# Residual of the S5 output tiles added by the copying engine, with a new task order

## The chip, the cores and the metric

The kernel runs on one core of a Trainium2 chip. A core has five engines that take their own instruction queues in order: TensorE (PE, matrix products; its weight loads are shown apart as PEld), VectorE (DVE), ScalarE (ACT), GpSimd (POOL) and SyncE (SP), which here only issues DMA transfers. Engines wait for each other through semaphores. Products land in PSUM, eight banks of 512 fp32 numbers for each of 128 partitions; DVE and ACT copy them from there to SBUF, the working memory.

The metric is the device time of one execution in microseconds. Three runs of the kernel before gave 341.81, 342.16 and 343.07; the median is 342.16.

## What is computed

One sequence of 2048 tokens with 640 channels passes four layers: A, B, A, B. Weights are shared between the two A layers and between the two B layers, and B's inputs k and v are given, not computed from x.

```
x = x + A(layernorm(x))      # S5: h_t = Lam*h_{t-1} + B u_t ; y = 2 Re(C h_t) + D*u
x = x + B(layernorm(x))      # H3: kv = shift_conv(k)*v ; y = q*(fft_conv(kv, ssm_k) + kv*ssm_D)
x = x + A(layernorm(x))
x = x + B(layernorm(x))
```

In A, u is the normalised x, h a complex state of 640 channels, and the last step of a tile adds three things: the product of state and output matrix, the skip term D*u, and the residual x. In B, q is the normalised x, and the long convolution does not depend on x, so it is computed once for both layers. The output is bf16.

## The kernel before, in words

**Stages.** The first part of the kernel prepares: tables for the Fourier transforms (`yt_`), the products k*v (`kv_`), the S5 matrices in two forms for even and odd steps (`a_b0`, `a_b1`, `a_w1`, `a_wc`, `a_wm`, tables `a_t`), and five passes over 128 channels each, `yq0` to `yq4`, that compute B's convolution: forward transform of kernel (`KA`, `KB`) and data (`VA`, `VB`), a product on DVE (`pw`), and the inverse (`IB`, `IA`), with transposes by DMA (`vl`, `tt`) between. The result goes to a DRAM scratch `ysd` (`st`). Each of these products is an `m` task on PE with an `e` task beside it that copies the bank out.

Then the layers A1, B1, A2, B2 work on four chunks `c0` to `c3` of 512 tokens. An A chunk has these tasks:

- `ln_*`, `id:q` normalise, `tu` transposes by DMA;
- `bq`, `bp` multiply by B for odd and even steps (PE), `eq`, `ev` copy out;
- `ri` turns the phases so that the scan becomes real, `sc` scans, `cy` hands the state to the next chunk, `ro` turns back, `hx` forms the even states: all on DVE, all strictly one after another;
- `cp:q` is the output product of one tile of 128 tokens (PE, two banks), `xe:q` copies it out into `x` and sums it for the next layernorm.

The last chunk (`QUADS`) handles four tokens at a step, with shorter scans and additional small products `b4` and `h1` and their copies `e2` and `eh`. `a_tq`, `a_rq` and `a_lamd2` make its tables. A B chunk has `ln_*`, `u` (normalise), `mm` (multiply by the convolution), `m` (add the residual) and, in B2, `st` (store).

**The residual of a tile.** Chunks of A1 reload x in bf16 (`xr`); chunks of A2 have it in SBUF in fp32. `PE_RES` lists the chunks of A1 and `XE32` the chunks of A2 where PE adds it: `e_cp` then ends each of its two column groups (512 and 128) with a product of an identity with x, in bf16 for A1 and in fp32 for A2's last chunk. These are all four chunks of A1 and chunk 3 of A2. For such tiles `e_xe` is a plain copy with a running sum, on ACT (line 900) or on DVE (line 902). For the chunks 0 to 2 of A2 `e_xe` is always on DVE and adds x in the same instruction (line 904).

**The order.** Nothing is scheduled at run time. `ORDER` is a list of 907 task names, written out by an earlier planner; `Sched.run` emits them one by one, so the list is the order of every engine's queue, SP's among them. A letter behind a name picks the engine where there is a choice (`/a` ACT, `/d` DVE, `/p` POOL). `PLACE` gives each buffer its place in one large SBUF arena (units of 64 bytes) or its PSUM bank; a buffer may overlap an earlier one, whose readers it then waits for. The estimates beside the tasks do not affect the emitted program.

**Warm-up.** `e_warm` fills PE's time before its first input with 72 products of the identity with itself, 128 columns each.

Of the kernel before, what the change touches and what calls it, by code (L numbers as in the profile page):

```python
# [9 lines left out]
ALU = mybir.AluOpType  # L10
# [7 lines left out]
P = 128  # L18
L = 2048
D = 640  # L20
# [15 lines left out]
PE_RES = (0, 1, 2, 3)  # L36
QUADS = (3,)
XE32 = (3,)
# [20 lines left out]
ORDER = """  # L59
warm yt_io8 yt_ph8 a_ldB0 yq0_kl a_ldB1 a_b00:4 kv_kd a_pl kv_dsl kv_lk0 kv_lv0 a_b00:1 a_b00:2 yt_sin8 yt_f0 kv_pd2/p  # L60
a_ti yt_h0 kv_pd0/d yt_f2 yt_f3 yt_io0 yt_h1 yq1_kl kv_lk1 xl0 kv_lv1 yt_ph0 kv_pd1/d kv_d0 a_p0 yt_neg8 kv_pd4/d
kv_k0 yt_f4 a_p1 yt_sin0 a_b0e0:4/a yt_neg0 a_p2 a_b0e0:1/a a_b00:3 kv_k1 kv_d1 a_b01:3 yt_h2 a_p3 a_b0e0:2/d a_dd
a_b0e1:3/a a_b0e0:3/d kv_d2 kv_k2 yq0_ka kv_ds0 kv_ds2 kv_ds4 kv_ds3 kv_ds1 yt_h3/p kv_pd3/p a_b01:2 a_b01:0
a_b0e1:0/a a_b0e1:2/d a_b00:0 a_b0e0:0/a a_p4a a_p4 yq0_KA:m0 yq0_KA:m3 yq0_KA:m1 kv_mm0:1 yq0_KA:e1/d yq0_KA:e0/a
yq0_KA:e3/a a_p5a yq0_KA:m2 yq0_KA:e2/a kv_ev0:1 a_ta a_p5b a_b01:4 a_b0e1:4/d kv_mm0:0 yq0_KB:m2 kv_ev0:0 yq1_ka
yq0_KB:e2/d yq1_KA:m2 a_t0 yq1_KA:e2/a yq0_KB:m0 yq1_KA:m3 yq0_KB:m3 yq0_KB:e0/a yq1_KA:e3/a yq0_vl a_ldC0 yq1_KA:m1
yq1_KA:e1/a a_ldC1 yq0_KB:e3/d a_p6 a_lamd yt_Si yt_Ci xl2 kv_lk2 kv_lv2 yq2_kl a_b01:1 kv_mm1:1 kv_ev1:1 a_b0e1:1/a
kv_mm1:0 kv_ev1:0 a_t1 yq1_vl kv_lk3 yq0_KB:m1 a_b11:1 a_b1e1:1/d a_b11:0 a_b10:1 kv_lv3 a_b11:3 a_b1e0:1/a a_b1e1:3/a
yq0_KB:e1/d a_b1e1:0/a A1c0_ln_bn:3/d yq0_VA:m2 yq0_VA:e2/d yq0_VA:m3 yq0_VA:m1 yq0_VA:e1/d yq0_VA:e3/a yq0_VA:m0
a_b11:4 a_b1e1:4/d yq0_VA:e0/a yq1_KA:m0 a_f A1c0_ln_bn:1/d A1c0_ln_bn:0/d a_b10:4 yq1_KA:e0/a a_b1e0:4/a yq0_VB:m0  # L70
a_ct1 yq0_VB:m3 yq0_VB:e0/a a_wc01:0 a_wm01:0 yq0_VB:e3/a yq0_VB:m2 yq0_VB:e2/a a_lm2 yt_nsi yt_nci a_wc01:1 a_wm01:1
a_b10:2 yq0_VB:m1 a_b1e0:2/a yq0_VB:e1/a yq0_pw:0 yq1_KB:m1 a_b10:3 yq1_KB:e1/a yq1_KB:m3 a_b1e0:3/a a_b11:2 a_b10:0
yq1_KB:m2 a_b1e1:2/a a_b1e0:0/a yq1_KB:e2/a yq1_KB:e3/a kv_mm2:1 yq0_IB:m1 yq0_IB:m0 kv_mm2:0 A1c0_ln_bn:2/d
A1c0_ln_sd A1c2_ln_bn:0/d kv_ev2:1 yq2_ka A1c0_ln_post A1c0_id:0/d yq0_IB:e1/a A1c0_id:1/d kv_ev2:0 yq1_KB:m0 a_t2
A1c0_id:2/d yq0_IB:e0/a A1c0_id:3/a yq1_KB:e0/a yq2_KA:m3 yq1_VA:m2 yq0_IB:m3 yq2_vl yq2_KA:m0 yq2_KA:e3/a yq1_VA:e2/a
yq2_KA:e0/d yq1_VA:m1 yq1_VA:m0 A1c2_ln_bn:3/d A1c2_ln_bn:1/d A1c2_ln_bn:2/d yq0_IB:e3/a yq1_VA:m3 yq0_IB:m2
yq1_VA:e0/a yq1_VA:e1/a yq1_VA:e3/a kv_mm3:1 kv_ev3:1 yq0_IB:e2/a yq0_tt A1c2_ln_sd a_ct4 yq1_VB:m1 kv_mm3:0 a_wc04:0
a_wm04:0 A1c2_ln_post yq1_VB:e1/a yq1_VB:m0 a_wc04:1 yq1_VB:e0/a kv_ev3:0 a_wm04:1 yq1_VB:m3 a_ct0 yq1_VB:e3/d
A1c2_id:2/a a_wc00:0 a_wm00:0 A1c2_id:0/d A1c2_id:3/d A1c2_id:1/d yq1_VB:m2 yq1_VB:e2/a a_wc00:1 a_wm00:1 yq0_IA:m1
yq0_IA:e1/a A1c0_tu xl1 yq0_IA:m0 yq2_VA:m3 yq0_IA:e0/a yq1_pw:0 yq0_st yq2_VA:m2 yq2_VA:e3/a yq2_KA:m1 yq2_KA:m2  # L80
yq3_kl kv_lv4 kv_lk4 yq2_VA:e2/a a_ct2 yq2_KA:e1/a yq2_KA:e2/a a_wc02:0 a_wm02:0 yq2_VA:m1 yq3_vl yq2_KB:m0
A1c1_ln_bn:2/d yq2_VA:e1/a yq2_KB:m1 yq2_KB:e0/a a_wc02:1 a_wm02:1 yq1_IB:m0 yq2_KB:e1/a yq1_IB:e0/a A1c1_ln_bn:1/d
yq2_VA:m0 yq2_VA:e0/a A1c1_ln_bn:3/d yq3_ka A1c1_ln_bn:0/d yq1_IB:m3 yq1_IB:e3/a a_ct3 a_wc03:0 yq1_IB:m1 yq1_IB:e1/a
a_wm03:0 yq1_IB:m2 yq1_IB:e2/d yq1_tt A1c1_ln_sd a_wc03:1 a_wm03:1 yq2_KB:m2 yq2_KB:e2/a kv_mm4:1 yq3_KA:m2 kv_mm4:0
yq2_VB:m2 yq3_KA:e2/a yq3_KA:m0 A1c1_ln_post A1c1_id:1/d kv_ev4:1 yq2_VB:m0 A1c1_id:3/a yq3_KA:e0/a kv_ev4:0
yq2_VB:e2/d yq2_KB:m3 yq3_KA:m1 A1c1_id:2/d yq2_VB:m1 yq2_KB:e3/d A1c1_id:0/d yq2_VB:e0/a yq3_KA:e1/d A1c0_bq:2
yq2_VB:m3 yq2_VB:e1/a A1c0_eq:2/a yq3_KA:m3 yq3_VA:m0 A1c0_bp:2 A1c2_tu yq3_KA:e3/d yq2_VB:e3/a yq1_IA:m1 yq2_pw:0
A1c0_bq:1 yq3_VA:e0/a A1c0_ev:2/a yq1_IA:e1/a xl3 A1c0_eq:1/a yq4_kl A1c1_tu yq4_vl A1c3_ln_bn:1/d yq3_KB:m0 yq3_VA:m1
yq3_VA:m2 A1c0_bp:1 yq3_VA:e1/a yq3_VA:e2/a yq3_VA:m3 A1c0_ev:1/d yq3_KB:m3 A1c3_ln_bn:3/d yq4_ka A1c3_ln_bn:0/d
yq3_KB:e0/a yq3_VA:e3/a yq2_IB:m2 yq3_KB:e3/a yq3_KB:m2 yq2_IB:e2/a yq3_KB:e2/a yq3_VB:m2 yq3_VB:e2/a yq2_IB:m0  # L90
yq2_IB:e0/d yq3_VB:m3 yq3_VB:e3/a yq1_IA:m0 yq1_IA:e0/d yq1_st A1c3_ln_bn:2/d yq3_VB:m0 yq4_KA:m2 yq2_IB:m1 yq3_KB:m1
yq3_VB:e0/a yq4_KA:e2/d yq2_IB:m3 yq2_IB:e1/a A1c3_ln_sd yq3_VB:m1 yq2_IB:e3/d A1c3_ln_post A1c3_id:0/d yq3_KB:e1/a
yq3_VB:e1/a A1c3_id:3/d yq3_pw:0 A1c3_id:1/d yq4_KA:m3 yq4_KA:e3/a A1c0_bq:0 yq2_tt yq4_KA:m1 yq4_KA:m0 A1c1_bq:0
A1c0_eq:0/a A1c3_id:2/a yq4_KA:e0/a yq4_KA:e1/a A1c0_bp:0 a_rq A1c0_ev:0/a yq4_KB:m1 A1c2_bq:2 yq3_IB:m3 A1c0_ri
A1c0_sc a_rq2 A1c0_cy A1c0_ro yq4_KB:e1/a yq2_IA:m0 A1c2_eq:2/a A1c1_bq:2 A1c2_bp:2 A1c1_eq:0/a yq3_IB:e3/a
yq2_IA:e0/a yq2_IA:m1 A1c2_ev:2/a A1c1_eq:2/a yq2_IA:e1/a A1c1_bq:1 A1c1_eq:1/a yq2_st A1c1_bp:2 yq4_KB:m2 A1c1_bp:1
yq4_KB:e2/a yq4_VA:m3 yq4_VA:e3/a A1c1_ev:2/a A1c1_ev:1/a A1c1_bp:0 yq3_IB:m1 yq3_IB:m2 A1c1_ev:0/a yq4_VA:m1
yq3_IB:e1/a yq4_KB:m3 yq4_VA:e1/a yq3_IB:m0 A1c2_bq:0 yq3_IB:e2/d A1c1_ri A1c0_hx A1c1_sc A1c1_cy yq3_IB:e0/a
yq4_VA:m2 yq4_VA:m0 yq4_KB:e3/a A1c2_eq:0/a A1c2_bq:1 yq4_VA:e0/a yq4_KB:m0 A1c3_tu A1c0_xr yq4_VA:e2/a A1c2_eq:1/a
yq4_VB:m3 A1c2_bp:0 yq3_tt yq4_VB:e3/a yq4_VB:m1 yq4_KB:e0/a A1c2_ev:0/a yq4_VB:m0 yq4_VB:m2 A1c2_bp:1 yq4_VB:e2/d  # L100
A1c1_xr yq4_VB:e1/a yq4_VB:e0/d yq4_pw:0 A1c0_cp:1 A1c1_ro A1c2_ev:1/a A1c0_xe:1/a a_w10:2 a_w1e0:2/a a_w11:0 a_w10:1
a_w11:4 A1c0_cp:3 a_w1e1:4/a a_w1e0:1/a a_w1e1:0/a yq4_IB:m2 a_w11:3 a_w10:3 A1c0_xe:3/a a_w10:0 yq4_IB:e2/a yq4_IB:m0
a_w1e0:3/a a_w1e1:3/a a_w1e0:0/d yq4_IB:e0/a a_w11:2 yq4_IB:m1 a_w10:4 a_w1e1:2/a yq4_IB:e1/a yq4_IB:m3 a_w1e0:4/d
a_w11:1 yq4_IB:e3/a yq3_IA:m1 yq3_IA:e1/d a_w1e1:1/d A1c1_hx yq4_tt A1c2_ri A1c1_cp:3 A1c1_xe:3/a yq3_IA:m0 A1c0_cp:0
yq3_IA:e0/a A1c3_bq:2 yq4_IA:m1 A1c0_xe:0/a yq4_IA:e1/a A1c0_cp:2 A1c0_xe:2/a A1c3_eq:2/d A1c2_sc A1c2_cy A1c2_ro
yq4_IA:m0 yq4_IA:e0/a B1c0_ln_nm B1c0_ln_sq:2 B1c0_ln_sq:1 A1c1_cp:1 A1c1_xe:1/a B1c0_ln_sq:0 B1c0_ln_sq:3 A1c1_cp:0
yq3_st A1c2_xr yq4_st B1l0 A1c1_cp:2 B1c0_ln_sd B1c0_ln_post B1c0_u:3/d A1c1_xe:0/d A1c2_hx B1c0_u:2/d B1c0_u:0/a
A1c1_xe:2/a B1c1_ln_nm B1c1_ln_sq:3 B1c1_ln_sq:2 B1c1_ln_sq:0 B1c1_ln_sq:1 B1c0_u:1/d B1c0_mm B1c0_m:3 B1c0_m:1
A1c3_bq:0 A1c3_bp:2 A1c2_cp:1 A1c3_bq:1 B1c0_m:2 B1c0_m:0 B1c1_ln_sd B1c1_ln_post a_lamd2 B1c1_u:0/d B1c1_u:1/d
A1c3_eq:0/a A2c0_ln_nm A2c0_ln_sq:1 B1c1_u:3/a B1l2 B1l1 A1c3_bp:0 B1c1_u:2/d B1c1_mm B1c1_m:0 A1c2_xe:1/d  # L110
A2c0_ln_sq:0 A1c3_eq:1/a A2c0_ln_sq:3 A1c3_bp:1 A1c3_e2:2/a A1c3_e2:0/a A2c0_ln_sq:2 A2c0_ln_sd B1c1_m:1 A1c3_b4:2
A1c3_b4:0 A1c2_cp:3 B1c1_m:3 A2c0_ln_post B1c1_m:2 A2c0_id:0/a A1c3_e2:1/a A2c1_ln_nm A1c3_ev:0/d A2c0_id:3/d
A2c0_id:2/d A1c3_ev:2/a A2c0_id:1/a A1c3_b4:1 A2c1_ln_sq:3 A2c0_tu a_tq/d A1c3_ev:1/a A1c3_ri A1c3_sc A1c3_ro
A1c3_hx:1 A1c3_xr A1c2_cp:2 A1c2_xe:3/a A2c1_ln_sq:1 A2c1_ln_sq:0 A1c2_cp:0 A1c2_xe:2/a A2c1_ln_sq:2 A1c2_xe:0/a
B1c2_ln_nm B1c2_ln_sq:2 B1c2_ln_sq:0 B1c2_ln_sq:3 B1c2_ln_sq:1 B1c2_ln_sd B1c2_ln_post B1c2_u:0/d B1c2_u:1/d A2c0_bq:1
A2c0_bq:2 A2c0_eq:1/a A1c3_h1:1 A2c0_bq:0 A1c3_h1:0 A1c3_h1:2 B1c2_u:3/a A2c0_bp:1 B1c2_u:2/d B1c2_mm B1c2_m:1
A1c3_eh:1/d A1c3_eh:0/d B1c2_m:3 A1c3_eh:2/a A2c1_ln_sd A2c0_eq:0/a A2c0_eq:2/a A2c0_ev:1/a A2c0_bp:0 A2c1_ln_post
# [77 lines left out]
    "A2c2_pb0": 6, "A2c2_pb1": 0, "A2c2_pb2": 4, "A2c2_pc0": 6, "A2c2_pc1": 2, "A2c2_pc2": 4, "A2c2_pc3": 0,  # L195
    "A2c3_pb0": 6, "A2c3_pb1": 4, "A2c3_pb2": 2, "A2c3_ph0": 0, "A2c3_ph1": 1, "A2c3_ph2": 6, "A2c3_pc0": 4,
    "A2c3_pc1": 6, "A2c3_pc2": 0, "A2c3_pc3": 2,
}


class Task:
# [1340 lines left out]
```

## Time and profile before

| | before |
|---|---|
| median of 3 runs | 342.16 us |
| profiled execution | 345.72 us |
| its span, first to last instruction | 343.6 us |
| PE busy | 318.2 us (93%) |
| DVE busy | 315.8 us (92%) |
| ACT busy | 248.8 us (72%) |
| POOL busy | 15.3 us (4%) |
| mean granted PE clock | 0.97 |
| DMA moved | 41.6 MB |

The profiled execution is one more run, a little slower than the others; its span leaves out 2.1 us at the ends. A row of a view names the engine, the source line, the operation, output and input, and a count; "busy" of PE counts every product until its modelled end, so that back-to-back products overlap and the start times tell the true rate. The waits are put down to the last releaser. ACT's largest waits are those for the output products, 20.9 us in 11 waits before line 900.

### The profile page before, as it was taken

To read this page: it belongs to the slowest core of one execution; us is meant where nothing else is said; L and a number is where in the kernel's file an instruction comes from. 1 tells how busy PE (TensorE), PEld (TensorE's weight loads), DVE (VectorE), ACT (ScalarE), POOL (GpSimd) and SP (SyncE) were. 2 spreads that over 40 slices of the span, in tenths; PEclk is the share of its full clock that TensorE was granted. 3 is DMA by queue.
4 is the path that set the end of the run, shared out by engine and by line. 5 is a ranking of instruction groups with operands and counts; after the bars stand their busy time and mean duration, and the time that the engine had idled before them with its cause. 6 is when DMAs were issued, how large, how long until landed. Compare 5 with 4: busy or idle time off the path is not lost. (4 is left out here: it accounts for less than half of the span.)

```text
span 343.6 us, 9079 instructions
## 1 busy us (share of the span) xinstructions
PE 318.2 (93%) x3924; PEld 250.9 (73%) x3924; DVE 315.8 (92%) x469; ACT 248.8 (72%) x401; POOL 15.3 (4%) x51
## 2 busy tenths in 40 slices
PE   7776989958899999999999999999999999999992
PEld 7666889857788889887666677676677786776551
DVE  6997997989889899999879999999998999999995
ACT  6897899989779797883745687888474783580772
POOL 6640000000000000000000000000000000000000
PEclk9897899987999999999999999999999999999998
DMA  8999998599959752078064550611416040224023
GB/s 210 242 201 254 228 208 156 100 214 217 189 98 188 166 110 63 2 129 226 0 118 88 167 184 0 155 32 46 88 66 78 3 76 2 76 78 154 2 112 117
DMA packets 105097, 41.61 MB, mean 121 GB/s; under 512 B 97885, under 2 KB 100450, under 8 KB 105058
## 3 DMA queue, kind: packets, MB, share of 16 engines
q1 hardware_dynamic: 104912, 41.03, 55.3%
q8 instruction: 30, 0.49, 0.6%
q14 instruction: 9, 0.07, 0.1%
q10 hardware_dynamic: 146, 0.01, 0.0%
HBM read 19.02 MB, written 5.24 MB: 71 GB/s over the span
## 5 line engine op out<-in xcount | busy, mean ns | idle before, releaser
L288 ACT ACTIVATE arena<-banks 128x1024 bf16<-128x1024 f32 (+3 forms) x155 | 135.3, 921 | 50.7 <-PE banks L756 13.1
L892 PE MATMUL banks<-arena 128*128 128x128 bf16 (+1 forms) x800 | 102.7, 283 | 0.4 <-DVE arena L902 0.4
L892 PEld LDWEIGHTS <-arena 128*128 128x128 bf16 x800 | 61.3, 98 | 42.6 <-issue 2.8
L741 PE MATMUL banks<-arena 128*128 128x256 bf16 x400 | 47.0, 273 | 0.2 <-DMA arena<-arena 0.2
L756 PE MATMUL banks<-arena 128*128 128x256 bf16 x400 | 46.9, 273 | 0.0
L290 DVE CAST arena<-banks 128x1024 bf16<-128x1024 f32 (+3 forms) x35 | 36.2, 1048 | 9.9 <-PE banks L1254 3.2
L756 PEld LDWEIGHTS <-arena 128*128 128x128 bf16 x400 | 38.6, 98 | 4.7
L741 PEld LDWEIGHTS <-arena 128*128 128x128 bf16 x400 | 38.3, 98 | 4.8 <-issue 0.4
L794 DVE TENSOR_TENSOR arena<-arena 128x5160 bf16<-128x5160 bf16 (+1 forms) x16 | 40.2, 2510 | 1.4 <-PE banks L892 1.0
L633 ACT ACTIVATE junk<-arena,nmean 128x640 bf16<-128x640 f32 x48 | 39.6, 826 | 1.1
L1276 PE MATMUL banks<-arena 128*128 128x256 bf16 x160 | 38.5, 279 | 1.3 <-ACT arena L288 1.0
L811 DVE TENSOR_TENSOR_SCAN arena<-arena 128x1290 bf16<-128x1290 f32 (+1 forms) x16 | 39.3, 2498 | 0.2
L1277 PE MATMUL banks<-arena 128*128 128x128 bf16 x160 | 35.7, 223 | 2.9 <-issue 2.9
L1278 PE MATMUL banks<-arena 128*128 128x128 bf16 x160 | 35.7, 223 | 0.0
L687 ACT ACTIVATE arena<-arena,nmr,rstd 128x640 bf16<-128x640 f32 (+1 forms) x25 | 22.4, 912 | 7.6 <-DVE nmr L646 7.1
L900 ACT ACTIVATE arena<-banks 128x640 f32<-128x640 f32 x18 | 12.6, 701 | 21.1 <-PE banks L892 20.9
L1358 PE MATMUL banks<-arena 128*128 128x128 bf16 (+1 forms) x288 | 24.1, 237 | 0.0
L1358 PEld LDWEIGHTS <-arena 128*128 128x128 bf16 x288 | 20.8, 98 | 1.8
L795 DVE TENSOR_TENSOR arena<-arena 128x2580 bf16<-128x2580 bf16 (+1 forms) x16 | 21.4, 1336 | 0.6
L1278 PEld LDWEIGHTS <-arena 128*128 128x128 bf16 x160 | 16.0, 100 | 5.3 <-issue 3.0
L689 DVE TENSOR_SCALAR arena<-arena,rstd,nmr 128x640 bf16<-128x640 f32 (+1 forms) x35 | 18.0, 550 | 0.4
L1277 PEld LDWEIGHTS <-arena 128*128 128x128 bf16 x160 | 15.9, 100 | 1.8 <-issue 1.7
(207 smaller groups left out, 441.5 us busy)
## 6 DMA issues: line engine op xcount, KB each, us to landing
arena<-in_A_x_dram SPq DMA_DIRECT2D x8, 640.0 KB, 4.6
arena<-ysd SPq DMA_DIRECT2D x8, 640.0 KB, 5.0
arena<-in_B_ssm_k_dram SPq DMA_DIRECT2D x5, 512.0 KB, 6.9
arena<-in_B_v_dram SPq DMA_DIRECT2D x5, 512.0 KB, 6.8
ysd<-arena SPq DMA_DIRECT2D x5, 512.0 KB
out_dram<-arena SPq DMA_DIRECT2D x8, 320.0 KB, 2.2
arena<-in_A_B_re_dram SPq DMA_DIRECT2D x1, 800.0 KB, 5.2
arena<-in_A_B_im_dram SPq DMA_DIRECT2D x1, 800.0 KB, 6.8
```

Source lines behind the costliest of these rows:

```text
L288: nc.scalar.activation(out, in_, ACT.Copy)
L290: nc.vector.tensor_copy(out, in_)
L633: nc.scalar.activation(small.junk, src(q), ACT.Square, bias=st["nmean"][:, i:i + 1], scale=1.0, accum_out=st["ssq"][:, i:i + 1])
L741: nc.tensor.matmul(pb[:, jj, c2, :], lhsT=bt0[:, c2, k, j * P:(j + 1) * P], rhs=uT[:, 2:4, k, :], start=(c2 == k == 0), stop=(c2 == 1 and ...
L756: nc.tensor.matmul(pb[:, jj, c2, :], lhsT=bt1[:, c2, j, k, :], rhs=uT[:, 0:2, k, :], start=False, stop=(c2 == 1 and k == NJ - 1), skip_gro ...
L794: nc.vector.tensor_tensor(tt, gs[:, :, None].to_broadcast([P, 2, 2, n]), by_pairs(tab.get().rearrange("p i j b -> p (i j b)"), n), ALU.mult)
L811: nc.vector.tensor_tensor_scan(gv, rt, gv, 0.0, ALU.mult, ALU.add)
L892: nc.tensor.matmul(pc[:, o0:o1], lhsT=lh, rhs=rh, start=(n == 0), stop=(n == len(ops) - 1))
L1276: nc.tensor.matmul(ps[:, g], lhsT=T["Cf"].get()[:, q, :], rhs=A[:, 2 * q:2 * q + 2, :], start=True, stop=False, skip_group_check=True)
L1277: nc.tensor.matmul(ps[:, g, 0, :], lhsT=T["Sf"].get()[:, q, :], rhs=aim, start=False, stop=False, skip_group_check=True)
L1278: nc.tensor.matmul(ps[:, g, 1, :], lhsT=T["NSf"].get()[:, q, :], rhs=are, start=False, stop=True, skip_group_check=True)
L1358: nc.tensor.matmul(ps[:, bi + b0:bi + b1, :], lhsT=T[tb].get()[:, q, :], rhs=rh, start=(n == 0), stop=(n == len(ops) - 1), skip_group_chec ...
```

## The change

The two lists `PE_RES` and `XE32` go. Whether PE adds the residual is now decided for each tile by the engine letter of its `xe` task: a tile that ACT copies gets the identity products (bf16 in A1, fp32 in A2), a tile that DVE copies gets none, and DVE adds x in the copy. Both layers and all chunks may now use either engine. The warm-up is 18 products of 512 columns in place of 72 of 128. `ORDER` and `PLACE` are new throughout: the same 907 tasks in another order, with other letters at some of them and other places.

```diff
-PE_RES = (0, 1, 2, 3)
-XE32 = (3,)
...
+ENG = dict(w.split("/") for w in ORDER.split() if "/" in w)
...
-        pe32 = reload is None and c in XE32
-        on_pe = pe32 or (reload is not None and c in PE_RES)
+        pe32 = reload is None
...
+            on_pe = ENG.get(f"{nm}_xe:{q}", "d" if pe32 else "a") == "a"
...
             def e_xe(eng, q=q, s_pc=s_pc):
-                if on_pe and eng == "act":
+                if eng == "act":
                     nc.scalar.activation(s_x[q].get(), s_pc.get()[:, 0:D], ACT.Identity, accum_out=sums_out()[:, q:q + 1])
-                elif on_pe:
-                    nc.vector.tensor_scalar(s_x[q].get(), s_pc.get()[:, 0:D], 1.0, 0.0, ALU.mult, ALU.add, accum_out=sums_out()[:, q:q + 1])
                 else:
                     nc.vector.scalar_tensor_tensor(s_x[q].get(), s_pc.get()[:, 0:D], 1.0, resid(q), ALU.mult, ALU.add,
                                                    accum_out=sums_out()[:, q:q + 1])
...
-        for i in range(72):
-            nc.tensor.matmul(s_warm.get()[:, P * (i % 4):P * (i % 4 + 1)], lhsT=consts["ident_bf"][:], rhs=consts["ident_bf"][:], start=True, stop=True)
+        for i in range(18):
+            nc.tensor.matmul(s_warm.get().rearrange("p (a n) -> p a n", n=P), lhsT=consts["ident_bf"][:], rhs=consts["ident_bf"][:, None, :].to_broadcast([P, 4, P]), start=True, stop=True)
```

Of the new order, the stretch of A1c1's output tiles:

```
A1c1_xe:3/d A1c2_sc A1c0_cp:2 A1c2_xr yq3_st A1c0_xe:0/d A1c0_xe:2/d yq4_IA:m1 A1c3_bp:2 yq4_IA:m0 B1c0_ln_nm
yq4_IA:e1/a yq4_IA:e0/a yq4_st B1l0 B1c0_ln_sq:0 B1c0_ln_sq:2 B1c0_ln_sq:3 B1c0_ln_sq:1 B1c0_ln_sd A1c2_cy A1c1_hx
a_lamd2 A1c2_ro A1c1_cp:1 A1c1_cp:2 A1c1_cp:0 B1c0_ln_post B1c0_u:3/a B1c0_u:0/a B1c0_u:1/a A1c1_xe:2/d A1c1_xe:1/d
A1c3_bq:0 A1c3_bq:1 A1c1_xe:0/d B1c1_ln_nm B1c1_ln_sq:1 A1c3_e2:2/a B1c1_ln_sq:2 B1c1_ln_sq:3 B1c1_ln_sq:0 B1c1_ln_sd
```

its end, from the last S5 chunk's rotation:

```
A2c3_b4:0 A2c2_cp:2 A2c2_xe:1/d B2c1_u:1/d A2c3_ev:0/a B2c1_u:2/a B2c1_u:0/a A2c3_ri A2c2_xe:2/d A2c3_sc A2c3_ro
A2c2_cp:3 A2c2_xe:3/d A2c2_cp:0 B2c1_mm B2c1_m:3 A2c3_hx:1 B2c1_m:0 B2c1_m:1 A2c2_xe:0/a A2c3_h1:0 A2c3_h1:2 A2c3_h1:1
A2c3_eh:0/a B2c2_ln_nm B2c2_ln_sq:1 A2c3_eh:2/a B2c2_ln_sq:2 B2c2_ln_sq:0 A2c3_eh:1/a B2c1_m:2 B2c2_ln_sq:3 B2c2_ln_sd
A2c3_cp:3 A2c3_xe:3/d B2c33_ln_nm B2c33_ln_sq:3 A2c3_cp:2 A2c3_hx:0 B2c2_ln_post B2c2_u:1/d B2c33_u:3 B2c2_u:2/a
```

and the stretch around the load `xl1`:

```
kv_mm2:0 a_b10:3 a_b10:0 yq1_KB:e2/a a_b1e0:3/a yq1_KB:m3 a_b11:2 a_b1e0:0/a kv_mm2:1 kv_ev2:1 xl1 A1c0_id:1/d
kv_ev2:0 A1c2_ln_bn:0/d A1c2_ln_bn:3/d A1c1_ln_bn:0/d A1c1_ln_bn:2/d A1c1_ln_bn:3/d yq1_vl A1c0_id:3/d A1c2_ln_bn:2/d
A1c0_id:2/d kv_lk3 yq2_vl yq1_KB:e3/a yq1_KB:m0 yq2_KA:m3 a_b1e1:2/a A1c0_id:0/a yq1_KB:e0/a yq2_KA:e3/a yq0_IB:m0
```

Counts that the letters give: of the 32 `xe` tasks 18 are on ACT before and 5 after (A1c0:1, A1c3:0, A2c2:0, A2c3:0, A2c3:1), 14 on DVE before and 27 after.

## The prediction

> **What bounds the kernel now.** I read the busy times by stretch first, cut at the first S5 rotation (126.8 us), at the last one's start (about 310) and at the last product (337). The columns are the stretch, its length, then busy us (and instruction count) of PE, PEld, DVE, ACT and POOL, the granted clock, the DMA share and GB/s.
>
> ```profile
> 0.00:126.80 126.80, 109.84 (x1983) 97.35 (x1984) 112.15 (x215) 107.88 (x143) 15.28 (x51) 0.93 0.96 188
> 126.80:337.00 210.20, 208.32 (x1943) 153.54 (x1941) 200.52 (x250) 138.79 (x254) 0.00 (x0) 1.00 0.32 81
> 309.00:343.60 34.60, 27.59 (x212) 16.57 (x209) 30.61 (x48) 15.71 (x39) 0.00 (x0) 0.95 0.26 95
> ```
>
> From 126.8 to 337 us PE is idle for 1.9 us and DVE for 9.7. ACT is idle for 71. So PE sets the pace there, with DVE 4% behind it; ACT has room. In the first stretch no engine is full, DMA is (0.96). A busy PE row can hide waits, so I checked it in the timeline by starts: one S5 output tile (start, length, what) is
>
> ```profile
> 217.74 2.54 PE L892 MATMUL banks<-arena 128*128 128x512 bf16 x14
> 220.12 0.38 PE L892 MATMUL banks<-arena,ident_bf 128*128 128x512 bf16 x1
> 220.34 0.78 PE L892 MATMUL banks<-arena 128*128 128x128 bf16 x11
> 220.95 0.22 PE L892 MATMUL banks<-arena,ident_bf 128*128 128x128 bf16 x1
> 221.01 3.44 PE L741 MATMUL banks<-arena 128*128 128x256 bf16 x30
> ```
>
> From start to start: 3.27 us a tile, no holes. The two identity products take 220.34-220.12 = 0.22 and 221.01-220.95 = 0.06, together 0.27 (unrounded). A tile of A2's last chunk carries them in fp32:
>
> ```profile
> 328.36 2.54 PE L892 MATMUL banks<-arena 128*128 128x512 bf16 x14
> 330.74 1.08 PE L892 MATMUL banks<-arena,ident_f 128*128 128x512 f32 x2
> 331.66 0.78 PE L892 MATMUL banks<-arena 128*128 128x128 bf16 x11
> 332.27 0.44 PE L892 MATMUL banks<-arena,ident_f 128*128 128x128 f32 x2
> ```
>
> 0.92 + 0.28 = 1.19 us (the next tile starts at 332.55). A tile without identity, as in A2's first chunks, is 75 + 25 products: three in 8.99 us, 3.00 each.
>
> The chain of waits, from 213 us on, runs almost wholly over DVE, changes to PE for the last four tiles and ends on DVE:
>
> ```profile
> 320.15 16.76 PE banks L892 x116
> ...
> 339.48 0.89 DVE arena L942
> ```
>
> **Removed from PE.** I count engine letters in the order. Of A1's 16 tiles 14 now go to DVE (A1c0:1 and A1c3:0 stay on ACT): 14 x 0.27 = 3.8 us. In A2 the fp32 identity leaves A2c3:2 and A2c3:3 and comes new to A2c2:0: 1.19 us net. In sum 5.0 us. Up to A2c3_b4:0, the last product that its rotation waits for, both orders hold the same PE tasks (one tile of A2c2 done, three to come), so only the 3.8 counts on the way there.
>
> **Moved from ACT to DVE.** A copy with residual on DVE, and one on ACT:
>
> ```profile
> 262.49 0.82 DVE L904 SCALAR_TENSOR_TENSOR arena<-banks,arena 128x640 f32<-128x640 f32 x1
> 263.23 0.08 DVE L904 DVE_READ_ACCUMULATOR arena<-banks,arena 128x1 f32 x1
> 263.23 0.82 DVE L974 SCALAR_TENSOR_TENSOR arena<-arena 128x640 f32<-128x640 bf16 x1
> ...
> 241.32 0.70 ACT L900 ACTIVATE arena<-banks 128x640 f32<-128x640 f32 x1
> 241.92 0.19 ACT L900 ACTIVATION_READ_ACCUMULATOR arena<-banks 128x1 f32 x1
> 242.01 0.70 ACT L900 ACTIVATE arena<-banks 128x640 f32<-128x640 f32 x1
> ```
>
> By starts 0.75 on DVE, 0.69 on ACT. The two tiles that DVE now copies without residual take 818 ns, those with it 816, so the added operand is free. Its bf16 form from a bank is in no row; the nearest, L974 with a bf16 operand from SBUF, has the same 0.82. Thirteen tiles move, net: +9.7 us on DVE, 9.0 off ACT. The Trainium skill ("VectorE: DVE Perf Modes", Specifications) speaks against the direction: VectorE sits closer to SBUF, ScalarE closer to PSUM. The rows put that at 0.06 us a tile, 0.8 for thirteen, off an engine with 71 us to spare; what matters is that the receiving engine has little. So the order gives other work back. Up to A2c3's rotation DVE gets 12 tiles (+9.0) and three more setup copies (+2.2, at 0.735 by starts), and loses a_tq (2.2), three W1 copies (2.4), and net four A2 and two B1 normalisations (6 x 0.53) and two or three A1/A2 copies (about 2): net +1.4 of some 280 us. Split at A1's first rotation it is about +3.3 before, where DVE idles 14.6, and -1.9 after. After A2c3_ro DVE's list shrinks from 22.1 us (318.3 to 340.4) to 21.0: one fewer copy of A2c2, plus two of A2c3, minus the two eh copies and one of B2's normalisations.
>
> **Warm-up.** 72 x 128 and 18 x 512 are the same 9216 columns; before they take 5.8 us. Bounds: the wide form one microsecond later or earlier for the first setup product, in a stretch where ACT and DVE are still in the sine tables; 0 taken.
>
> **Order and places.** 907 tasks each, the same set. Costs from both sides: the orders share their broad shape, and a place only shows as a wait. What I can check: in SP's queue xl1 moves ahead of yq1_vl and kv_lk3. It overwrites B's imaginary half (its place 469 lies in 452-552), so it waits for a_b11:2, and yq1_vl, whose place overlaps the same slot and kT2, stands behind it. Before, yq1_vl was issued at 45.2; now it follows kv_mm2, near 55, and takes 4.8 us of SP, while PE has 5.5 us of listed work between kv_mm2 and the product that needs it: 0 to 2 us of waiting. I take 0, since PE idles 17 us in the first 100 anyway; SP's other moves (xl3 and A1c0_tu earlier, yq0_st later) have slack of the same kind.
>
> **The end.** After A2c3_b4:0 before needs 343.6-309.0 = 34.6 us. After, on DVE: 1.0 to the rotation, 2.5 rotation, 0.75 (A2c2_xe:2 now between), 3.4 scan, 2.4 back, 21.0, 3.2 for the store = 34.2. On PE: two tiles 6.0 and one of 4.2 up to the h1 products, just within those 10; then 1.7 + 6.0 + 8.4 + 6.6 = 22.7 against DVE's 24.2. So DVE ends it, and of PE's 1.2 only 0.4 arrives.
>
> **Sum.** -3.8 - 0.4 = -4.2 if PE keeps its density. I give back 0.6, because DVE must fit its 173 us between first and last rotation into 178 instead of 182. Forecast **-3.6**. It is made against the profiled execution, 345.72 us of which 343.6 are span; the median of the runs is 342.16, and I carry the difference over: **338.6 us**.
>
> **Rivals.**
> 1. *DVE becomes the bound.* For it: DVE is in the chain of waits from 213 on, and its list grows by 1.4. Against it: its idle time there is waiting for PE. If DVE keeps its idle time: +1.4 - 0.4 = +1.0, **343.2**.
> 2. *Banks held by DVE* (slower). DVE takes its queue in order, and its scan pair (5.6) and rotation (4.4) cannot be passed. Place: A1c1. Its tiles cp:1, cp:2, cp:0 are listed ahead of a_lamd2, A1c2_ro and a post on DVE (6.8 us after hx), then xe:2. A1c3_bq:0 needs banks 2-3, and xe:2 frees 1-2: it can start 7.7 us after hx, PE is there after 6.0. So 1.7 us; before, ACT freed these within 1 us. If it happens at five chunks, 8.5: 342.2 - 4.2 + 8.5 = **346.5**. It decides from 5.9 us of new PE waits on. Against: the other copies are listed close behind their tiles.
> 3. *A hole in the front end.* If yq1_vl makes PE wait longer, the clock adds to it. Before has one such hole:
>
> ```profile
> 30.51 0.27 PE L1277 MATMUL banks<-arena 128*128 128x128 bf16 x1 [2.87 <-issue]
> 30.57 0.31 PE L1278 MATMUL banks<-arena 128*128 128x128 bf16 x1
> 30.68 0.42 PE L1276 MATMUL banks<-arena 128*128 128x256 bf16 x1
> ```
>
> After it products start 107 ns apart instead of 55, until 34.2: 1.8 us lost. "TensorE: Matmul & The Clock Gate" (Part 1) names an idle window of about 3.4 us; by that a 2.9 us hole is free, by the row it costs 1.8. I take the row: 3.0 (640 KB at 220 GB/s) + 1.8 - 4.2: **342.8**.
> That the identities stay is excluded by the code: `on_pe` follows the letter, and five tiles keep ACT.
>
> **Chances.** Forecast 0.60 (own range 335.5 to 340.4), rivals 0.14, 0.18 and 0.08. Range: down to 334.5, if DVE's idle time shrinks and the front end gains a few us of its own 17; up to 346, all but the far half of rival 2. Runs of this kernel tell 0.5%, 1.7 us, from nothing: faster is below 340.5, slower above 343.9. Forecast 0.57 faster, 0.03 same; rival 1 0.03, 0.08, 0.03; rival 2 all but 0.01 slower; rival 3 0.03, 0.04, 0.01. Rounded: faster 0.63, same 0.16, slower 0.21.
>
> **What would show it.** Right: identity products of 512 columns fall from 16 to 2 in bf16 and from 8 to 6 records in fp32; ACT's sum-copies from 18 to 5, DVE's from 14 to 27; PE near 99% busy from 127 us to its end, DVE's idle time there below 9.7; A1c0's rotation near 127. Wrong: PE rows with a wait on L904's successor (rival 2), DVE without idle time while PE has holes (1), PE's clock under 0.9 in 40 to 80 us (3).

## The result, and the profile after

The changed kernel takes **341.25 us** (median of 20 runs, 340.52 to 343.10). The kernel before, run beside it, took 342.99 (20 runs). The ratio is **0.9947, 95% interval 0.9928 to 0.9967**: 1.7 us, half a per cent, is gained. The forecast was 338.6, so about half of the predicted 3.6 us came. Four executions of this study, at 347.78, 414.56, 534.03 and 819.05 us, took over 1.5% longer than the fastest of the same kernel, and medians and ratios leave them out.

The rotations of the eight S5 chunks are good marks. Each begins with the memset of line 798 on DVE, and between the marks one can see where time came and went. The kernel before was profiled twice more in the study, because the execution shown ahead of the prediction took longer than the others.

| us | before, shown above | before, again (two runs) | after (two runs) |
|---|---|---|---|
| time of the profiled execution | 345.72 | 342.80, 342.39 | 341.21, 341.34 |
| first rotation (A1c0) | 126.8 | 124.4, 124.1 | 127.7, 127.9 |
| first to last rotation (A2c3) | 183.3 | 182.7, 182.6 | 178.7, 178.7 |
| last rotation to the end | 33.5 | 33.6, 33.6 | 33.0, 33.0 |

The first and the last mark of a repeated run of before, and then those of the kernel after:

```profile
124.39 0.07 DVE L798 MEMSET arena<- 128x10 uint32 x1
307.11 0.07 DVE L798 MEMSET arena<- 128x10 uint32 x1 [0.22 <-ACT arena L288]
```

```profile
127.73 0.07 DVE L798 MEMSET arena<- 128x10 uint32 x1 [0.39 <-ACT arena L288]
306.44 0.07 DVE L798 MEMSET arena<- 128x10 uint32 x1
```

So two things happened. From the first rotation on, the changed kernel takes 211.6 or 211.7 us where the repeated kernel before takes 216.2 or 216.3, so it is 4.5 to 4.7 us faster; ahead of it, it is 3.5 us slower. The execution shown ahead of the prediction hides the second: its own front happened to be 2.5 us late, and against it the new first rotation looks unmoved.

The busy times by stretch answer to those shown before. The first three rows are of the kernel after, cut at its first and last rotation; the last is the middle stretch of a repeated run of the kernel before. The columns are again stretch, length, busy us and count of PE, PEld, DVE, ACT and POOL, granted clock, DMA share and GB/s.

```profile
0.00:127.73 127.73, 110.69 (x1929) 93.52 (x1930) 115.73 (x220) 105.71 (x139) 19.32 (x52) 0.93 0.95 187
127.73:306.44 178.71, 178.18 (x1711) 135.17 (x1709) 171.49 (x219) 127.02 (x211) 0.00 (x0) 1.00 0.34 86
306.44:339.40 32.96, 25.15 (x203) 15.47 (x200) 28.93 (x45) 16.60 (x40) 0.00 (x0) 0.91 0.19 73
```

```profile
124.39:307.11 182.72, 181.64 (x1739) 137.50 (x1737) 173.98 (x212) 126.05 (x222) 0.00 (x0) 1.00 0.35 80
```

In the middle PE is busy for 178.2 of 178.7 us: it still sets the pace, with 3.5 us less to do. DVE has 171.5 us of work in place of 174.0, so the thirteen copies that it took over were more than paid back by work taken off it. In the front DVE has 115.7 us of work, where the repeated run of before had 112.0, 3.7 us more; the prediction counted +3.3.

The costliest groups by shape show the change itself: busy us, mean ns of one, and the idle time before them.

```profile
L892 PE MATMUL banks<-arena,ident_f 128*128 128x512 f32 x6 | 3.2, 620 | 0.0
L892 PE MATMUL banks<-arena,ident_bf 128*128 128x512 bf16 x2 | 0.8, 379 | 0.0
L900 ACT ACTIVATE arena<-banks 128x640 f32<-128x640 f32 x5 | 3.5, 699 | 12.7 <-PE banks L892 12.7
L902 DVE SCALAR_TENSOR_TENSOR arena<-banks,arena 128x640 f32<-128x640 f32 x27 | 21.5, 817 | 0.1
```

Of those with 512 columns, 2 identity products in bf16 and 6 records in fp32 are left, 5 copies on ACT and 27 on DVE, as counted. The bf16 residual that no row of before showed costs DVE nothing more: all 27 copies, 14 of them with a bf16 residual, last 799 to 824 ns.

### The profile page after: what moved, and what is told of

It is laid out like the page before. It is cut to its first block, busy times and chain, and to the rows that moved or that the text cites. A ratio compares the mean times of both kernels' runs of the same rounds, so it can differ in the third digit from the quotient of the medians.

```text
span 339.4 us, 8921 instructions
## 1 busy us (share of the span) xinstructions
PE 314.0 (93%) x3838; PEld 244.1 (72%) x3838; DVE 316.1 (93%) x481; ACT 249.3 (73%) x388; POOL 19.3 (6%) x52
## 5 line engine op out<-in xcount | busy, mean ns | idle before, releaser
L288 ACT ACTIVATE arena<-banks 128x1024 bf16<-128x1024 f32 (+2 forms) x156 | 135.2, 914 | 36.3 <-PE banks L741 12.1
L892 PE MATMUL banks<-arena 128*128 128x128 bf16 (+1 forms) x800 | 99.4, 283 | 0.2 <-DVE arena L795 0.2
L290 DVE CAST arena<-banks 128x1024 bf16<-128x1024 f32 (+3 forms) x34 | 35.1, 1055 | 10.5 <-PE banks L1275 4.7
L687 ACT ACTIVATE arena<-arena,nmr,rstd 128x640 bf16<-128x640 f32 (+1 forms) x32 | 28.4, 912 | 12.5 <-DVE nmr L646 12.3
L1275 PE MATMUL banks<-arena 128*128 128x128 bf16 x160 | 35.8, 224 | 0.0
L1274 PE MATMUL banks<-arena 128*128 128x128 bf16 x160 | 35.8, 224 | 0.0
L1355 PE MATMUL banks<-arena 128*128 128x128 bf16 (+1 forms) x288 | 24.3, 238 | 0.3 <-DVE arena L484 0.3
L795 DVE TENSOR_TENSOR arena<-arena 128x2580 bf16<-128x2580 bf16 (+1 forms) x16 | 21.4, 1337 | 0.5
L902 DVE SCALAR_TENSOR_TENSOR arena<-banks,arena 128x640 f32<-128x640 f32 x27 | 21.5, 817 | 0.1
L1251 PEld LDWEIGHTS <-arena 64*128 64x128 bf16 x320 | 11.1, 103 | 8.6 <-issue 5.4
```

The costliest lines, as they stand in the source:

```text
L288: nc.scalar.activation(out, in_, ACT.Copy)
L290: nc.vector.tensor_copy(out, in_)
L892: nc.tensor.matmul(pc[:, o0:o1], lhsT=lh, rhs=rh, start=(n == 0), stop=(n == len(ops) - 1))
L1274: nc.tensor.matmul(ps[:, g, 0, :], lhsT=T["Sf"].get()[:, q, :], rhs=aim, start=False, stop=False, skip_group_check=True)
L1275: nc.tensor.matmul(ps[:, g, 1, :], lhsT=T["NSf"].get()[:, q, :], rhs=are, start=False, stop=True, skip_group_check=True)
L1355: nc.tensor.matmul(ps[:, bi + b0:bi + b1, :], lhsT=T[tb].get()[:, q, :], rhs=rh, start=(n == 0), stop=(n == len(ops) - 1), skip_group_chec ...
```

## The experiments

### The same kernels again, and the identities put back

First the kernels before and after were run once more, and the changed kernel was given back the identity products on the tiles that DVE copies (DVE then copies without adding, as before). Order and places stay those of the change.

```diff
-            on_pe = ENG.get(f"{nm}_xe:{q}", "d" if pe32 else "a") == "a"
+            on_pe = reload is not None or c in QUADS or ENG.get(f"{nm}_xe:{q}", "d" if pe32 else "a") == "a"
...
+                elif on_pe:
+                    nc.vector.tensor_scalar(s_x[q].get(), s_pc.get()[:, 0:D], 1.0, 0.0, ALU.mult, ALU.add, accum_out=sums_out()[:, q:q + 1])
```

The expectation for the repeated kernel before:

> The kernel before, unchanged, profiled once more. Theory 1 (the recorded execution of before was a slow one of its kind, late already at the first S5 rotation, because the DMA-bound first part varies): the span is near 341 us, the first rotation (the first memset of line 798) starts near 124 and from there to the end it takes 216.8 us as in the first record. Theory 2 (the surplus lay in the S5 part): the first rotation starts at 126.8 again and the rest takes some 2.5 us less. Theory 3: 343.6 and 126.8 again, and profiled executions are all slower than timed ones.

and for the identities put back:

> The kernel after, with the identity products put back on all 16 tiles of A1 and all four of A2's last chunk (DVE then copies without adding); order and places as after. PE gets 14 x 0.27 + 2 x 1.19 = 6.2 us of work back, DVE's work is the same. If PE sets the pace of the S5 part (my prediction): slower than after by 3.8 up to the last rotation plus up to 2.4 behind it, 345 to 347 us. If DVE already sets it after the change: less than 2 us slower, 341.5 to 343.

Measured with the identities: 346.15 us, ratio to before 1.0088 (1.0058 to 1.0118), 4.8 us above the repeated run of the changed kernel (341.34). The first rotation stays (127.5 us); first to last rotation takes 181.7 us instead of 178.7, and the rest 34.6 instead of 33.0. Removing the products from PE is thus worth 4.6 to 4.8 us within the new order, all of it behind the first rotation. It shows that PE sets the pace there. From the first rotation on this kernel takes 216.3 us, as the kernel before does, although it has one pair of fp32 identity products more (that of A2c2:0). Of the 3.8 us that 14 bf16 tiles should give, 3.0 are seen up to the last rotation; of the 2.4 us of two fp32 tiles, 1.6 behind it.

### Front and S5 part exchanged

The orders of both kernels hold the same PE tasks up to A1c0_bp:0, the last product ahead of the first rotation. So they can be cut there and joined crosswise, with one buffer moved in each.

In the first kernel the list begins with the 408 tasks of the kernel before up to A1c0_bp:0, with their letters and places, and goes on with what is left of the changed kernel's list. The join, against the kernel before:

```diff
 A1c0_eq:0/a A1c3_id:2/a yq4_KA:e0/a yq4_KA:e1/a A1c0_bp:0
-a_rq A1c0_ev:0/a yq4_KB:m1 A1c2_bq:2 yq3_IB:m3 A1c0_ri
+a_rq a_rq2 A1c0_ev:0/a yq4_KB:m1 yq4_KB:e1/a A1c2_bq:2 A1c1_eq:0/a A1c2_eq:2/a A1c0_ri
...
-"A1c1_uT": 1418
+"A1c1_uT": 1419
```

> The changed kernel with the front of the kernel before: the order, letters and places of the kernel before up to A1c0_bp:0, those of the changed kernel behind it (one place moved). Theory (the front lost 3.6 us, the S5 part gained 4.7, each by itself): first rotation near 124.2 us instead of 127.8, from there 211.7 to the end, so 341.3 - 3.6 = 337.7 us. Rival (the two are one: the new front hands the S5 part more finished work, so its gain needs it): from the first rotation 214 to 216 us, time 340 to 342.

Measured: **337.26 us, ratio to before 0.9835 (0.9793 to 0.9878)**. First rotation at 124.3 us, from there 211.3 to the end. Its stretches up to the first rotation, and from there to the last:

```profile
0.00:124.32 124.32, 106.78 (x1929) 91.39 (x1930) 111.95 (x217) 107.76 (x142) 15.28 (x51) 0.96 0.96 192
124.32:303.02 178.70, 177.06 (x1693) 135.05 (x1709) 171.49 (x221) 127.14 (x211) 0.00 (x0) 1.00 0.35 85
```

The opposite join has the kernel before behind the changed kernel's front:

> The kernel before with the front of the changed kernel, up to A1c0_bp:0 (identity products in all tiles of A1, as before; warm-up of 128 columns). Theory: first rotation near 127.8, from there 216.3, so 342.6 + 3.6 = 346.2 us. Rival (front and S5 part belong together): 342 to 344.

Measured: 346.31 us, ratio 1.0104 (1.0048 to 1.0160). Its profiled execution took 349.43 us, with 216.8 us from the first rotation to the end. Both medians and both times from the first rotation on lie within 0.6 us of what the theory expected. The first rotation of that profiled execution, at 130.8 us, can't be set against the expected 127.8, since the execution took 3.1 us longer than the median. By these marks the S5 part gains 4.5 to 5.2 us, behind either front, and by the ratios 5.4 to 5.7; the new front costs 3.5 us by the marks and 3.6 to 3.8 by the ratios. Neither needs the other. The first mixed kernel is also the fastest of this study, 1.1% below the changed kernel.

### The letters alone, in the old order

Is the new order needed for the gain? Here the `xe` tasks have the change's letters, the code is that of the change with its warm-up of 512 columns, and everything else is as before (one buffer moved). All 32 have the new letters, of which those of A1c1 are shown:

```diff
-A1c1_cp:3 A1c1_xe:3/a
+A1c1_cp:3 A1c1_xe:3/d
...
-A1c1_cp:1 A1c1_xe:1/a
+A1c1_cp:1 A1c1_xe:1/d
...
-A1c1_xe:2/a
+A1c1_xe:2/d
```

> The residual moved as in the change, by the new letters of the xe tasks alone, in the order and with the other letters and places of the kernel before (one place moved). PE loses 5.0 us of identity products, DVE gets 13 copies more (+9.0 us up to the last rotation) and is relieved of nothing. Theory (DVE is 4% behind PE, so it becomes the bound): the gain of 4.7 in the S5 part goes and more: from the first rotation to the end 216 to 224 instead of 211.7, time 342 to 350. Rival (fewer products on PE are enough, the new order adds nothing in the S5 part): from the first rotation 211.7 to 212.5, time 338 to 339.

Measured: **373.37 us, ratio 1.0897 (1.0863 to 1.0930)**. Far worse than even the theory said: from the first rotation (123.6) to the end 247.5 us instead of 211.7. PE's waits of over 1 us behind 124 us (line and what it waited for: us in total, times, longest); lines of this kernel stand 9 lower, so L893 is the residual copy on DVE, L902 in the change:

```profile
PE banks L883 <- DVE arena L893: 17.7, 2, 9.3
PE banks L732 <- DVE arena L893: 5.3, 1, 5.3
PE banks L523 <- DVE arena L893: 2.2, 1, 2.2
PE banks L1374 <- DVE arena L893: 1.2, 1, 1.2
```

The longest, in the timelines of DVE and PE:

```profile
223.29 1.51 DVE L785 TENSOR_TENSOR arena<-arena 128x2600 bf16<-128x2600 bf16 x1
...
226.17 2.91 DVE L802 TENSOR_TENSOR_SCAN arena<-arena 128x650 bf16<-128x650 f32 x2
229.12 1.51 DVE L785 TENSOR_TENSOR arena<-arena 128x2600 bf16<-128x2600 bf16 x1
...
232.28 0.82 DVE L893 SCALAR_TENSOR_TENSOR arena<-banks,arena 128x640 f32<-128x640 f32 x1
```

```profile
220.73 3.16 PE L883 MATMUL banks<-arena 128*128 128x512 bf16 x25
233.16 0.59 PE L883 MATMUL banks<-arena 128*128 128x512 bf16 x1 [9.26 <-DVE arena L893]
```

PE ends a tile near 224; the copy that frees the next tile's bank stands on DVE behind a whole rotation, scan and rotation back, and PE idles for 9.3 us. Together 26.4 us of PE time are lost to this one kind of wait, out of the 35.8 us that this kernel is behind the changed one from the first rotation on. With the holes the clock goes down too, to 0.74 from 220 to 240 us, and PE is busy for 183.5 us between the first and the last rotation, where the changed kernel needs 178.2. It is the second rival, banks held by DVE, at its full size. The same view of the changed kernel, from 127.7 us on, has only these rows:

```profile
PE banks L741 <- DVE arena L902: 0.2, 1, 0.2
PE banks L892 <- DVE arena L795: 0.2, 1, 0.2
```

So the new order, with its other letters, keeps the rival away: in the stretches shown ahead of the prediction it lists the copies close behind their tiles, ahead of the long chains or between their parts.

### Where the front loses

The earliest trace of lateness is yq0_vl, the first transpose of k*v, which is issued at 24.0 us after and at 21.4 before. Two kernels tested it.

The first has the 99 tasks of the kernel before up to yq0_vl, and then what is left of the changed kernel's list:

```diff
 yq0_KB:e0/a yq1_KA:e3/a yq0_vl
-a_ldC0 yq1_KA:m1 yq1_KA:e1/a a_ldC1 yq0_KB:e3/d
+a_p6 a_lamd a_f A1c0_ln_bn:1/d yq1_KA:m1
```

> The changed kernel with the order of the kernel before for its first 99 tasks only, up to the transpose yq0_vl. If the loss arises in the first 24 us (yq0_vl issued at 24.0 instead of 21.4) and is carried through: yq0_vl near 21.5, first rotation 125.3, time 338.8. If the early lateness is absorbed and the loss arises between 24 and 90 us: first rotation 127 or later, time 341.

The second is the changed kernel with one DVE task moved:

```diff
-a_t0 kv_mm0:0 a_p5b kv_ev0:0 yq0_vl
+kv_mm0:0 a_p5b kv_ev0:0 yq0_vl a_t0
```

> The changed kernel with a_t0 (2.7 us of DVE) moved behind kv_ev0:0, so that the product k*v reaches yq0_vl sooner. If DVE's order at 20 to 23 us is what makes yq0_vl late and that is carried through: yq0_vl at 22.8 instead of 24.0, time 341.3 - 1.2 = 340.1. If it is absorbed: 341.3, within 0.4.

Measured: 343.25 us for the first (ratio 1.0022, 0.9993 to 1.0052), although yq0_vl was issued at 22.1; its first rotation came at 129.8, two microseconds later than in the changed kernel, which was not explained. And 342.1 for the second (ratio 0.9968, 0.9950 to 0.9985), no gain on the changed kernel's 0.9947; where its yq0_vl came is not shown, since no ordinary execution of it was profiled. The first kernel shows that an early yq0_vl is not carried through to the first rotation.

The next mark is yq0_tt, the transpose between the two inverse steps of pass 0, which SP can issue only when all four copies of yq0_IB are done. It is issued at 62.4 us in the repeated run of before and at 64.8 after. In the timelines of DVE, SP and PE, first the changed kernel's:

```profile
59.65 0.39 DVE L689 TENSOR_SCALAR arena<-arena,rstd,nmr 128x640 bf16<-128x640 bf16 x1
61.34 1.23 DVE L290 CAST arena<-banks 128x1024 bf16<-128x1024 f32 x1 [1.30 <-PE banks L1251]
62.48 0.88 DVE L660 BATCH_NORM_STATS2 bs<-arena 128x6 f32<-128x320 bf16 x2
63.40 0.21 DVE L661 BATCH_NORM_AGGREGATE mv<-bs 128x2 f32<-128x12 f32 x1
63.52 1.17 DVE L290 CAST arena<-banks 128x1024 bf16<-128x1024 f32 x1
```

```profile
64.77 4.70 SPq L1368 DMA_TRANSPOSE arena<-arena  x1
```

```profile
58.96 1.94 PE L1355 MATMUL banks<-arena 128*128 128x256 bf16 x24
...
73.31 1.11 PE L1383 MATMUL banks<-HA,arena 128*128 128x64 bf16 x32 [2.03 <-DMA arena<-arena]
```

and SP's and PE's in the repeated run of before:

```profile
62.36 4.78 SPq L1371 DMA_TRANSPOSE arena<-arena  x1
```

```profile
70.44 1.11 PE L1386 MATMUL banks<-HA,arena 128*128 128x64 bf16 x32 [2.02 <-DMA arena<-arena]
```

The products of yq0_IB:m2 end at 60.9, but DVE copies them only at 63.5: ahead of that copy its queue has yq1_VA:e0, which waits 1.3 us for a product of its own, and a statistics pass of A1c1. PE then waits 2.0 us for the transposed data, and behind it the clock goes down. Four microseconds each, with PE's busy time, granted clock, DMA share and GB/s, first after and then the repeated run of before:

```profile
76.00:80.00 4.00, 3.21 (x46) 0.50 1.09 257
80.00:84.00 4.00, 3.69 (x31) 0.50 1.16 252
```

```profile
72.00:76.00 4.00, 2.58 (x34) 0.51 0.94 251
76.00:80.00 4.00, 4.00 (x42) 0.64 1.16 230
```

So neither the wait nor the low clock is new: the kernel before has a wait of 2.0 us at the same product, yq0_IA:m1. New is that PE reaches the product 2.9 us later (73.3 against 70.4), and that its own work ahead of it, the same tasks but for one more (`a_wc00:1`) in before, also ends 2.9 us later (71.3 against 68.4). The last of this work follows a copy of DVE, kv_ev3:0, in both kernels (line 1221 after, 1224 before):

```profile
68.79 0.27 PE L1273 MATMUL banks<-arena 128*128 128x256 bf16 x1 [0.81 <-DVE arena L1221]
```

```profile
65.94 0.27 PE L1276 MATMUL banks<-arena 128*128 128x256 bf16 x1 [0.20 <-DVE arena L1224]
```

Up to the end of that copy DVE has 63.5 us of work after and 58.3 before. The new order lists all four statistics passes of A1c1, about 1 us each, ahead of it; the old order lists them behind it. That DVE's queue as a whole is late here for this reason fits the numbers, but no run put these passes back, so it is not shown. What was tested is the single copy, put first with nothing else changed:

```diff
-yq1_VA:e0/d A1c1_ln_bn:1/d yq0_IB:e2/d yq0_tt
+yq0_IB:e2/d yq0_tt yq1_VA:e0/d A1c1_ln_bn:1/d
```

> The changed kernel with one place in the order altered: DVE copies yq0_IB:e2 (and SP issues yq0_tt) ahead of yq1_VA:e0 and A1c1_ln_bn:1 instead of behind them. In the trace of the changed kernel the products of yq0_IB:m2 end at 60.9 us and the copy starts at 63.5. Theory (this copy makes the transpose yq0_tt late, and PE waits 2.0 us for it and runs at half clock behind it): yq0_tt issued near 62.2 instead of 64.8, the wait of 2.0 us at 71 us goes, first rotation 124 to 126 instead of 127.8, time 337.6 to 339.3. Rival (the loss is spread over the front and the wait only moves): first rotation 127 or later, time 340.8 or more.

Measured: 339.50 us (338.58 to 340.38), ratio 0.9902 (0.9870 to 0.9934). In its profiled execution, of 338.58 us, the first rotation comes at 125.1 and 211.6 us follow. The timelines of DVE, SP and PE:

```profile
60.06 2.36 DVE L290 CAST arena<-banks 128x1024 bf16<-128x1024 f32 x2 [0.45 <-PE banks L1355]
```

```profile
61.37 5.43 SPq L1368 DMA_TRANSPOSE arena<-arena  x1
```

```profile
70.43 0.63 PE L1383 MATMUL banks<-HA,arena 128*128 128x64 bf16 x16 [0.29 <-DVE arena L290]
```

The transpose is issued 3.4 us earlier and the wait for it is gone; the clock still goes down, to 0.64 from 76 to 80 us and 0.93 behind it. Not all of it is the edit's: the products of yq0_IB:m2 end at 60.0 here and not at 60.9, mainly since PE did not wait for yq1_vl ahead of them, as it does for 0.6 us in the changed kernel's profile, and nothing ahead of them was edited. One place in one queue is worth 1.5 us by the ratios (0.9947 to 0.9902), and of the 2.6 us by the profiled executions about 1.7 if that 0.9 is taken off. It is won by removing a wait that the kernel before has too. So it makes up for part of the 3.5 us that the front loses, but is not shown to be where they arise; PE's own lateness of 2.9 us at this product was not isolated.

The queue step that the prediction had named, xl1 ahead of yq1_vl on SP, was undone too:

```diff
-kv_mm2:1 kv_ev2:1 xl1 A1c0_id:1/d
+kv_mm2:1 kv_ev2:1 yq1_vl xl1 A1c0_id:1/d
...
-A1c1_ln_bn:3/d yq1_vl A1c0_id:3/d
+A1c1_ln_bn:3/d A1c0_id:3/d
```

> The changed kernel with yq1_vl issued ahead of xl1 on SP, as the kernel before has it. This is the queue step that the prediction took at 0. If it is the front's loss: yq1_vl issued 3 us or more earlier than 50.3, first rotation 125, time 339. Theory (yq1_vl waits for kv_mm2, not for xl1; PE waits 0.6 us for it): yq1_vl within 1 us of 50.3, time 340.6 to 341.6.

Measured: 344.06 us, ratio 1.0028 (1.0015 to 1.0041), slower by 0.8% than the changed kernel. yq1_vl goes out at 50.39 us, as in the changed kernel (50.34), so xl1 did not hold it up. But DVE's statistics of A1c1 now wait for xl1's data, and with them all that stands behind in its queue:

```profile
58.38 0.89 DVE L660 BATCH_NORM_STATS2 bs<-arena 128x6 f32<-128x320 bf16 x2 [3.07 <-DMA arena<-in_A_x_dram]
...
65.25 1.17 DVE L290 CAST arena<-banks 128x1024 bf16<-128x1024 f32 x1
```

The same copy of yq0_IB:e2 comes at 65.25 instead of 63.52, yq0_tt at 66.5, and the first rotation at 129.5. The expected time was missed. It is not the transpose alone: PE waits 0.9 and 1.4 us for copies of DVE at 64.3 and 66.5 us, and its wait ahead of yq0_IA:m1 at 75.0 us, of 1.3 us, is put down to DVE and not to the transpose. When DVE's queue is later here, the kernel is slower.

### The same edit in the mixed kernel

In the mixed kernel's front PE also waits for yq0_tt, 2.5 us. The copy was moved there as well, from ACT to DVE, which needs the products yq0_IB:m2 earlier and so a different order on PE.

```diff
-yq0_IB:m3 yq2_vl yq2_KA:m0 yq2_KA:e3/a yq1_VA:e2/a yq2_KA:e0/d yq1_VA:m1 yq1_VA:m0
+yq0_IB:m3 yq0_IB:m2 yq2_vl yq2_KA:e3/a yq0_IB:e3/a yq1_VA:e2/a yq0_IB:e2/d yq0_tt yq1_VA:m1 yq1_VA:m0 yq2_KA:m0 yq2_KA:e0/d
...
-yq0_IB:e3/a yq1_VA:m3 yq0_IB:m2 yq1_VA:e0/a
+yq1_VA:m3 yq1_VA:e0/a
...
-kv_mm3:1 kv_ev3:1 yq0_IB:e2/a yq0_tt
+kv_mm3:1 kv_ev3:1
```

> The mixed kernel (front of before, S5 part of the changed one, 337.3 us) with the same edit: yq0_IB:m2 ahead of yq2_KA:m0, yq1_VA:m1 and m0 on PE, its copy on DVE instead of ACT and ahead of that engine's other copies. Theory: yq0_tt issued near 60.7 instead of 62.6, the wait of 2.0 us on PE goes and with it the half clock behind it (1.3 us): 334 to 335.5. Rival: the wait only moves, 336.8 or more.

Measured: 339.05 us, ratio 0.9885 (0.9854 to 0.9917), no faster than the mixed kernel itself (0.9835, 0.9793 to 0.9878) and probably slower; the theory's number was missed and the rival's met. yq0_tt goes out 1.2 us earlier and the wait for it is gone, but kv_mm3 now waits 1.9 us for a copy on DVE, whose queue has the statistics ahead of it; the first rotation comes at 126.7 instead of 124.3. The wait moved.

## Why the prediction was half right

**PE sets the pace from the first rotation on: right.** PE is busy for 178.2 of 178.7 us there, and the products put back cost 4.8 us.

**Removed from PE, 3.8 up to the last rotation: right in the sum, in part by luck.** The stretch shrinks by 4.0 us. But the identity products put back cost only 3.0 of them, so about 1.0 us came from the new order, which the sum had put down as a loss of 0.6. **DVE's net -1.9 us behind the first rotation**: 2.5. **The end, -0.4**: 0.6. By these steps the S5 part should have gained 3.6; it gained 4.5 to 4.7.

**Warm-up, 0 taken: right.** The mixed kernel has the wide warm-up ahead of the old front, and its first rotation comes at 124.3, as before (124.1 and 124.4).

**Order and places, "I take 0, since PE idles 17 us in the first 100 anyway": this step failed.** The new front costs 3.5 us, and these are what the forecast lacks. The move that the step looked at, xl1 ahead of yq1_vl, did not delay yq1_vl: it goes out at 50.3 us (the step said near 55), PE waits 0.6 us for it, within the 0 to 2 us allowed, and undoing the move made the kernel slower. 2.9 of the 3.5 us are there when PE reaches yq0_IA:m1; one copy two places earlier in DVE's queue wins 1.5 to 1.7 us back. Where the 2.9 us arise stays open. The reason given for 0 was wrong in kind. PE's idle time over a long stretch is no cover, since it is itself made of waits for other engines. Likewise the +3.3 us that the prediction counted on DVE ahead of the first rotation were held to lie in 14.6 us of idle time; but from 20 to 60 us DVE is busy for 39.1 of 40 us after (36.3 in the repeated run of before), so there was no idle time where the new order puts the work. No run took work off DVE in this stretch, so its cost by itself is argued and not shown.

**The base.** The sum was made against one profiled execution and carried to the median as a difference. That execution lost its extra time in the front: its first rotation was at 126.8 instead of 124.1 to 124.4. The hole that the prediction showed for its third rival is where it fell back. In one repeated run the same hole is shorter, and the products behind it start 55 ns apart:

```profile
29.76 0.22 PE L1277 MATMUL banks<-arena 128*128 128x128 bf16 x1 [1.76 <-issue]
```

The eight products behind (line 1254) come at 34.36 us there and at 37.36 in the execution that served as the base, where the spacing of 107 ns lasts until 36.2 us and not until 34.2, as the prediction read (its 1.8 us lost is then some 2.8, an estimate from half the 5.7 us at that spacing); at 61 us the base is still 2.4 us late. So the sign named for success, "A1c0's rotation near 127", was nearly met (127.7), and meant the opposite. From the first rotation on that execution (216.8) was as good a base as any. The median of three runs to which the forecast was carried, 342.16, is 0.8 us below that of twenty.

**The rivals.** DVE as the bound: no, PE has no holes. Banks held by DVE: the mechanism exists at 26 us in the old order, and 0.2 us of it is left in the new one; the 1.7 us that the prediction guessed at A1c1 did not come. The hole in the front end gave 342.8 and is the nearest of the three to what happened, in place though not in mechanism: PE is late in the front end with DVE's queue, and not through a load on SP.

## What to carry to other kernels

Moving work from an engine with room to one that takes a queue of long chains is a question of order first: the same letters gave 1.6% less time in the right order (behind the old front) and 9% more in the old one. When a whole order is replaced, do not book it at zero because an engine is idle on average: follow the few transfers that a later stage waits for back to the last copy ahead of each, and count what stands before that copy in its queue. Set each such wait beside the same wait in the old order: one that was always there can be worth removing, but it is not what the new order lost. Take the marks of the stages from more than one execution before a difference is built on them.

## What was not expected of the hardware

The clock of PE fell to half behind a single wait of 2.0 us. In the changed kernel that wait ends at 73.3 us; the granted clock is 1.00 until 74.0, 0.85 in the half microsecond behind it and 0.50 from there to 84.5. Two shorter waits, of 0.9 and 0.8 us, fall into the slow stretch and not ahead of it; one of 0.8 us lies 2.5 us ahead of the long one. Behind the hole near 28 us the kernel before shows both cases: 2.9 us and, in the second repeated run, 2.0 us were followed by half clock, 1.8 us in the first repeated run were not. "TensorE: Matmul & The Clock Gate" (Part 1) in the Trainium skill speaks of a free-running window of about 3.4 us, one of which has to be idle; here a wait of 2.0 us is enough. Half clock does not always cost time: two runs of the changed kernel had 0.61 and 0.53, or 0.80 and 0.77, of the clock at 12 to 16 and 16 to 20 us, and their first rotations lie 0.1 us apart.

POOL's twenty elementwise products of line 1190 took 9.0 us in the new front; the same twenty (line 1193) take 7.2 in the old one. That was not explained.
